# Rounding of the weights with two VectorE operations, loads spread over the first units, two buffers of scores

## The chip, the cores and the metric

The kernel runs on one core of a Trainium2 chip. The metric is the device time of one execution in microseconds (us), as the median of several runs. Engines are named as in the profile: PE (TensorE, matmuls; PEld is its weight load), DVE (VectorE), ACT (ScalarE), POOL (GpSimd), SP (SyncE, which issues all DMAs here).

## The reference

Attention in which each query keeps its 32 largest scores, then a feed-forward block with a gated activation. The weights come in 64-bit floats, everything else in 32-bit.

```python
B, H, S, D = 8, 8, 576, 64
scores = q @ k.T / sqrt(D)
kth = 32nd largest score of each row
attn = softmax(where(scores >= kth, scores, -1e9))
x = (attn @ v)                      # to (B*S, H*D) = (4608, 512)
g = x @ w_gate                      # (512, 1536)
val = x @ w_val                     # (512, 1536)
out = (g * sigmoid(g) * val) @ w_out   # (1536, 512)
```

## The kernel before, in words

**Units.** The attention is cut into 160 units (`units`): for each of 8 batches, five query tiles (four of 128 rows, the last of 64), each for four pairs of heads. A unit of the first four tiles holds two heads side by side (128 x 1152 scores; "full unit"); one of the last tile holds both heads on the two halves of the partitions (128 x 576; "one-head unit").

**Stages of a unit.** `scores` multiplies on PE into four PSUM tiles and ACT copies them to `sc` (L261, or L247 for one-head units). `select` finds the 32nd largest on DVE in four rounds of eight: MAX8 (L277), then MATCH_REPLACE8 (L281) that blanks the found eight in `rest`; a compare (L287) writes the penalty `e`. `penalize` adds `sc` to `e` on POOL (L299). `weigh` takes exp on ACT with the row sum `tot` (L308); `normalize` adds a small constant and inverts `tot` on DVE (L318, L320) and scales `e` on ACT (L323). `turn` transposes `e` on PE (L335, nine 128 x 128 transposes, in groups of 5 and 4 with a piece of other work between them) and ACT copies the result to `et` (L336). `values` multiplies with V on PE (L355, L364) and ACT copies to `xT` (L379).

**The loop.** One iteration of the last loop treats four units at once: top-k of unit n, scores of unit n+1, penalty and exp of unit n-1, transposes of unit n-2, product with V of unit n-3. The Q/K slabs of a pair are prepared (`fetch`, `prep`) two units ahead. Instructions run on each of PE, DVE, ACT and POOL in exactly the order in which the loop writes them: the end of the kernel ties each to the one before it on its engine. SP has its own queue of DMAs, in program order too.

**The feed-forward block** runs over 18 blocks of 256 rows (`feed`). It is cut into pieces (`piece`): four matmuls with w_gate or w_val (L418), or two with w_out (L452). `credit` lets 4.6 pieces into a full unit and 2.3 into a one-head unit, as far as rows are ready. What follows a product on ACT (`gate`: tanh, a halved copy, plus one, L436 to L438, called the tanh trio in the text; `value`: a copy, L443) and on POOL (L439, L444) waits in the lists `on_act` and `on_pool` and is written out at `flush`.

**Rounding of the weights.** PE multiplies weights that are rounded from 64-bit floats by integer operations on the two 32-bit words of each (`rounded`). There are 72 pieces of 128 x 256. `weights` runs them as a pipeline of steps; in each step one piece has its DMA issued (L96), another, three steps behind, passes POOL's clamp (L102) and ACT's scaling and Abs (L107, L109), another, four behind, two DVE operations (L114, L117) and POOL's add (L121), and one five behind the last DVE operation (L124). `rounding(k)` runs k steps; `need` runs as many as a product asks for. The loop calls it with 5 steps in units 0 to 9 and 4 after that.

**Buffers.** `sc` has three buffers (L229), `e` three, `rest` one, the DMA tiles `w` four, `m` three. Scores, transposes, slabs and products with V share a pool of five PSUM tiles (`ps_t`), in rotation.

**Start.** Before the loop come K and Q of pair 0, three rounding steps, K and Q of pair 1, then for all four pairs K, Q (where not loaded) and V.

Of the kernel before, what the change touches and what calls it, by code (L numbers as in the profile page):

```python
# [15 lines left out]
P = 128  # L16
# [4 lines left out]
BLK = 256  # L21
WP = 256
HUGE = 122880.0
LEAST = 3.4332275390625e-05


@with_exitstack
def kernel(
# [63 lines left out]
    def rounded(src, dst):  # L92

        n = dst.shape[1]
        w = ffn.tile([P, n, 2], I32, tag="w", name="w", bufs=4)
        nc.sync.dma_start(w[:], src.bitcast(I32).rearrange("p (f t) -> p f t", t=2))  # L96
        yield
        low, high = w[:, :, 0], w[:, :, 1]


        hi = conv.tile([P, n], FP32, tag="hi", name="hi")
        nc.gpsimd.tensor_scalar(  # L102
            hi[:], high.bitcast(FP32), HUGE, -HUGE, ALU.min, ALU.max
        )

        ulps = conv.tile([P, n], I32, tag="ulps", name="ulps")
        nc.scalar.mul(ulps[:], low.bitcast(U32), 2.0**-29)  # L107
        size = conv.tile([P, n], FP32, tag="size", name="size")
        nc.scalar.activation(size[:], hi[:], AF.Abs)  # L109
        yield  # L110

        hi = hi[:].bitcast(I32)
        bits = conv.tile([P, n], I32, tag="bits", name="bits")
        nc.vector.tensor_scalar(  # L114
            bits[:], hi, 3, 0x3FFFFFFF, ALU.logical_shift_left, ALU.bitwise_and
        )
        nc.vector.scalar_tensor_tensor(  # L117
            out=bits[:], in0=hi, scalar=-0x40000000, in1=bits[:],
            op0=ALU.bitwise_and, op1=ALU.bitwise_or,
        )  # L120
        nc.gpsimd.tensor_tensor(bits[:], bits[:], ulps[:], ALU.add)  # L121
        yield

        nc.vector.scalar_tensor_tensor(  # L124
            out=dst, in0=size[:], scalar=LEAST, in1=bits[:].bitcast(FP32),
            op0=ALU.is_ge, op1=ALU.mult,
        )

    def weights():

        pieces = []
        for f in range(0, DFF, WP):
            for src, dst in ((w_gate, wg), (w_val, wv)):
                for c in range(KC):
                    pieces.append((src[c * P : (c + 1) * P, f : f + WP], dst[:, c, f : f + WP]))
        for c in range(MC):
            for f in range(0, DM, WP):
                pieces.append((w_out[c * P : (c + 1) * P, f : f + WP], wo[:, c, f : f + WP]))
        pieces = [rounded(*p) for p in pieces]
        for n in range(len(pieces) + 5):  # L140
            for lag in (5, 4, 3, 0):
                if 0 <= n - lag < len(pieces):
                    next(pieces[n - lag], None)
            ready[0] = max(n - 4, 0)
            yield

    ready = [0]
# [2 lines left out]
    def rounding(n):  # L150
        for _ in range(n):
            next(weight, None)

    def need(n):

        while ready[0] < n:
            next(weight)
# [68 lines left out]
    def scores(n):  # L226
        b, qt, hp = units[n]
        slab = preps[b * NHP + hp]
        sc = work.tile([P, 2 * S], FP32, tag="sc", name="sc", bufs=3)  # L229
        halves = [slice(0, D), slice(D, P)]  # L230
        half = S // 2

        def bank():
            return ps_t.tile([P, 512], FP32, tag="t", name="s")


        if qt == J:
            banks = [bank() for _ in range(2)]
            for i, ps in enumerate(banks):
                for d in halves:  # L240
                    k0 = R + i * half
                    nc.tensor.matmul(  # L242
                        ps[d, 0:half], slab[d, S + R : S + 2 * R], slab[d, k0 : k0 + half]
                    )
            yield
            for i, ps in enumerate(banks):
                nc.scalar.copy(sc[:, i * half : (i + 1) * half], ps[:, 0:half])  # L247
        else:
            q0 = S + 2 * R + qt * P
            banks = []  # L250
            for i in range(2):
                for hh, d in enumerate(halves):
                    ps = bank()
                    banks.append((i + 2 * hh, ps))
                    k0 = (1 - hh) * R + i * half
                    nc.tensor.matmul(  # L256
                        ps[:, 0:half], slab[d, q0 : q0 + P], slab[d, k0 : k0 + half]
                    )
            yield
            for i, ps in banks:  # L260
                nc.scalar.copy(sc[:, i * half : (i + 1) * half], ps[:, 0:half])  # L261
        state[n] = dict(sc=sc)

    def select(n):

        nh = n_heads(units[n][1])
        sc = state[n]["sc"]
        m = small.tile([P, 2, TOP_K], FP32, tag="m", name="m")
        heads = [slice(t * S, (t + 1) * S) for t in range(nh)]
        rest = work.tile([P, 2 * S], FP32, tag="rest", name="rest", bufs=1)  # L270
        e = work.tile([P, 2 * S], FP32, tag="e", name="e", bufs=3)
        state[n] |= dict(m=m, e=e, heads=heads)
        cur = sc
        rounds = TOP_K // 8
        for r in range(rounds):
            for t, hs in enumerate(heads):
                nc.vector.max(m[:, t, 8 * r : 8 * r + 8], cur[:, hs])  # L277
            yield
            if r < rounds - 1:
                for t, hs in enumerate(heads):  # L280
                    nc.vector.match_replace(  # L281
                        rest[:, hs], m[:, t, 8 * r : 8 * r + 8], cur[:, hs], LOWEST
                    )
                cur = rest
                yield
        for t, hs in enumerate(heads):
            nc.vector.tensor_scalar(  # L287
                e[:, hs], sc[:, hs], m[:, t, TOP_K - 1 : TOP_K], FAR, ALU.is_lt, ALU.mult
            )
# [114 lines left out]
    def feed(kb):  # L404
# [7 lines left out]
        def product(w, s, then):  # L412
            ps = ps_f.tile([P, 2, BLK], FP32, tag="f", name="f")
            need(8 * s + (4 if w is wg else 8))
            for i in range(2):
                m = 2 * s + i
                for c in range(KC):
                    nc.tensor.matmul(  # L418
                        ps[:, i, :],
                        w[:, c, m * P : (m + 1) * P],  # L420
                        x[:, c, :],
                        start=(c == 0),
                        stop=(c == KC - 1),
                    )
                if i == 1:
                    on_act.append(lambda: then(ps))
                yield
# [20 lines left out]
        for t in range(BLK // P):  # L448
            ps = ps_f.tile([P, DM], FP32, tag="f", name="o_ps")
            for m in range(MC):  # L450
                need(8 * MS + 2 * m + 2)
                nc.tensor.matmul(  # L452
                    ps[:],
                    hs[m // 2][:, m % 2, t * P : (t + 1) * P],
# [51 lines left out]
    def run(steps):  # L506
        for _ in steps:
            pass

    load(0)  # L510
    rounding(3)
    load(1)
    for i in range(NHP):
        if i > 1:
            load(i)
        load_v(i)
    run(fetch(0))
    run(scores(0))
    run(fetch(1))
    credit = [0.0]  # L520
    no = iter(())
    over = {}
    for n in range(NU + 3):
        topk = select(n) if n < NU else no
        over[n - 1] = normalize(n - 1) if 0 <= n - 1 < NU else no
        nxt = scores(n + 1) if n + 1 < NU else no
        turned = turn(n - 2) if 0 <= n - 2 < NU else no
        ahead = fetch(n + 2) if n + 2 < NU else no
        if n < NU:
            credit[0] = min(credit[0] + (2.3 if units[n][1] == J else 4.6), 8.0)  # L530
        flush(on_act)
        if 0 <= n - 1 < NU:
            penalize(n - 1)
        run(over.pop(n - 2, no))
        flush(on_pool)
        if n >= 3:
            values(n - 3)
            b, qt, hp = units[n - 3]
            if qt == J and b + 1 < B:
                load_v((b + 1) * NHP + hp)  # L540
        next(nxt, None)
        next(topk, None)
        next(topk, None)
        rounding(1 + (n < 2 * NHP + 2))
        pieces(1)
        next(nxt, None)
        next(turned, None)
        flush(on_act)
        pieces(1)
        next(turned, None)  # L550
        flush(on_act)
        if 0 <= n - 1 < NU:
            weigh(n - 1)
        flush(on_pool)
        next(topk, None)
        next(topk, None)
        rounding(1)
        next(ahead, None)
        pieces(1)
        next(ahead, None)  # L560
        next(topk, None)
        rounding(1)
        next(over[n - 1], None)
        pieces(1)
        next(topk, None)
        rounding(1)
        next(over[n - 1], None)
        next(topk, None)
        next(topk, None)
        pieces(6)  # L570
    while piece():
        pass
# [48 lines left out]
```

## Time and profile before

| | |
|---|---|
| median of 3 runs | 1973.31 us (1972.61 to 1979.06) |
| the profiled execution | 1975.04 us |
| its span in the profile | 1973.2 us |
| busy PE | 1779.5 us (90%) |
| busy DVE | 1640.1 us (83%) |
| busy ACT | 1156.0 us (59%) |
| busy POOL | 773.0 us (39%) |
| mean granted PE clock | 0.942 |

The page cuts the span into 40 equal slices and gives the busy share of each engine in tenths, and the PE clock granted by the throttle in tenths of full speed. A row of the timeline gives start, length, engine, line, operation, output and inputs, the number of instructions merged into it, and in brackets the idle time before it and what ended that. A row of the waits gives who waited for whom: total us, times, longest.

### The profile page before, as it was taken

What the parts mean: (1) busy time and instruction counts of PE and PEld (TensorE: products, weight loads), DVE (VectorE), ACT (ScalarE), POOL (GpSimd) and SP (SyncE); (2) the same over time, 40 slices, a digit from 0 to 9 for tenths busy, and PEclk for the clock granted to TensorE, in tenths of its full rate; (3) what the DMA queues carried; (4) which work ended last, traced back from release to release, by engine and by line L of the source; (5) the groups of instructions that cost most, each with busy time, mean ns of one, the idle gap of its engine ahead of it and who ended that gap; (6) DMA issues with size and microseconds to landing.
All of it is one profiled execution on the core that took longest, in us unless ns stands there. A gap on an engine that the chain in (4) does not pass through costs nothing.

```text
span 1973.2 us, 29487 instructions
## 1 busy us (share of the span) xinstructions
PE 1779.5 (90%) x10144; PEld 1297.7 (66%) x10144; DVE 1640.1 (83%) x3708; ACT 1156.0 (59%) x2821; POOL 773.0 (39%) x686
## 2 busy tenths in 40 slices
PE   3444779989999999999999999989999999899899
PEld 1223655847686867686768686858686867586666
DVE  5999687998889998989799898998898988889700
ACT  3555455656575656666667566656675656565512
POOL 2555453424334434343434352434343434243412
PEclk6566789999999999999999999999999999999999
DMA  5222111100030002100030002000120002000000
GB/s 153 84 80 75 43 50 43 44 12 1 9 79 11 1 12 57 30 1 11 4 78 7 12 2 68 18 11 1 33 54 11 1 14 50 11 1 11 1 11 11
DMA packets 111253, 59.58 MB, mean 30 GB/s; under 512 B 89088, under 2 KB 97280, under 8 KB 111104
## 3 DMA queue, kind: packets, MB, share of 16 engines
q1 hardware_dynamic: 111104, 57.70, 11.1%
q8 instruction: 80, 1.31, 0.3%
q14 instruction: 69, 0.57, 0.1%
HBM read 48.23 MB, written 9.44 MB: 29 GB/s over the span
## 4 chain that ended last, share of the span: by engine, by line
PE 78%; DVE 13%; issue 3%; ACT 3%; POOL 2%; SPq 1%; DMA 1%; POOLq 0%; ACTq 0%; DVEq 0%
PE f L418 37%; PE o_ps L452 18%; PE av L364 7%; PE etps L335 6%; PE s L256 6%; DVE m L277 5%; DVE rest L281 4%; PE s L242 2%; PE av L355 1%; PE kqps L211 1%; DVE bits L117 1%; DVE e L287 1%; DVE bits L114 1%; ACT e L308 1%; POOL bits L121 1%
## 5 line engine op out<-in xcount | busy, mean ns | idle before, releaser
L299 POOL TENSOR_TENSOR e<-e,sc 128x1152 f32<-128x1152 f32 (+1 forms) x160 | 383.0, 2394 | 731.3 <-DVE e L287 487.1
L277 DVE MAX8 m<-rest 128x8 f32<-128x576 f32 x864 | 613.7, 747 | 2.2
L418 PE MATMUL f<-xT,wg 128*128 128x256 f32 x1728 | 423.1, 391 | 16.7 <-ACT xT L379 16.7
L281 DVE MATCH_REPLACE8 rest<-m,rest 128x576 f32<-128x576 f32 x576 | 423.9, 743 | 0.0
L418 PE MATMUL f<-xT,wv 128*128 128x256 f32 x1728 | 409.3, 384 | 0.0
L452 PE MATMUL o_ps<-wo,h 128*128 128x512 f32 x864 | 400.1, 599 | 4.4 <-DVE wo L124 4.4
L418 PEld LDWEIGHTS f<-xT,wg 128*128 128x128 f32 x1728 | 323.4, 194 | 89.7 <-issue 27.8
L336 ACT COPY et<-etps 128x512 f32<-128x512 f32 (+1 forms) x448 | 195.1, 477 | 305.8 <-PE etps L335 305.2
L418 PEld LDWEIGHTS f<-xT,wv 128*128 128x128 f32 x1728 | 321.0, 193 | 48.3 <-issue 9.9
L335 PE MATMUL etps<-ident,e 128*128 128x128 f32 (+1 forms) x1312 | 207.4, 289 | 122.2 <-ACT sc L261 70.5
L335 PEld LDWEIGHTS etps<-ident,e 128*128 128x128 f32 (+1 forms) x1312 | 168.0, 148 | 202.8 <-issue 99.1
L323 ACT ACTIVATE e<-e,tot 128x576 f32<-128x576 f32 x288 | 209.5, 770 | 133.7 <-DVE tot L320 133.7
L452 PEld LDWEIGHTS o_ps<-wo,h 128*128 128x128 f32 x864 | 153.6, 190 | 163.6 <-issue 156.0
L439 POOL TENSOR_TENSOR h<-h,half_g 128x512 f32<-128x512 f32 x108 | 137.9, 1277 | 265.3 <-ACT h L438 258.8
L308 ACT ACTIVATE e<-e,bias 128x576 f32<-128x576 f32 x288 | 221.6, 776 | 4.1 <-POOL e L299 4.1
L277 DVE MAX8 m<-sc 128x8 f32<-128x576 f32 x288 | 205.1, 749 | 10.1 <-ACT sc L261 10.1
L281 DVE MATCH_REPLACE8 rest<-m,sc 128x576 f32<-128x576 f32 x288 | 212.0, 743 | 0.0
L256 PE MATMUL s<-kqT 64*128 64x288 f32 x1024 | 172.7, 459 | 11.4 <-ACT kqT L216 11.3
L364 PE MATMUL av<-et,v 128*64 128x128 f32 (+1 forms) x2560 | 178.5, 281 | 2.1 <-ACT et L336 1.0
L261 ACT COPY sc<-s 128x288 f32<-128x288 f32 x512 | 167.2, 416 | 12.8 <-PE s L256 12.3
L318 DVE TENSOR_SCALAR tot<-tot 128x2 f32<-128x2 f32 (+1 forms) x160 | 25.4, 159 | 168.0 <-ACT e L308 168.0
L444 POOL TENSOR_TENSOR h<-h,val 128x512 f32<-128x512 f32 x108 | 139.1, 1288 | 60.7 <-ACT val L443 60.3
(45 smaller groups left out, 1459.8 us busy)
## 6 DMA issues: line engine op xcount, KB each, us to landing
kq_in<-in_k_dram SPq DMA_DIRECT2D x64, 128.0 KB, 2.8
kq_in<-in_q_dram SPq DMA_DIRECT2D x64, 128.0 KB, 3.0
v<-in_v_dram SPq DMA_DIRECT2D x32, 256.0 KB, 3.0
w<-in_moe_w_gate_dram SPq DMA_DIRECT2D x24, 256.0 KB, 2.7
w<-in_moe_w_val_dram SPq DMA_DIRECT2D x24, 256.0 KB, 2.7
w<-in_moe_w_out_dram SPq DMA_DIRECT2D x24, 256.0 KB, 2.5
out_dram<-o SPq DMA_DIRECT2D x40, 128.0 KB, 2.4
out_dram<-o SPq DMA_DIRECT2D x16, 256.0 KB, 2.4
```

The lines of the kernel that those rows point to most:

```text
L256: nc.tensor.matmul(ps[:, 0:half], slab[d, q0 : q0 + P], slab[d, k0 : k0 + half])
L261: nc.scalar.copy(sc[:, i * half : (i + 1) * half], ps[:, 0:half])
L277: nc.vector.max(m[:, t, 8 * r : 8 * r + 8], cur[:, hs])
L281: nc.vector.match_replace(rest[:, hs], m[:, t, 8 * r : 8 * r + 8], cur[:, hs], LOWEST)
L299: nc.gpsimd.tensor_tensor(e[:, every], e[:, every], sc[:, every], ALU.add)
L308: nc.scalar.activation(e[:, hs], e[:, hs], AF.Exp, bias=bias[:, t : t + 1], scale=scale, accum_out=tot[:, t : t + 1],)
L323: nc.scalar.mul(e[:, hs], e[:, hs], tot[:, t : t + 1])
L335: nc.tensor.transpose(ps[0:kl, c * P : (c + 1) * P], e[:, k0 : k0 + kl], ident[:])
L336: nc.scalar.copy(et[0:kl, c0 : c0 + cn, :], ps[0:kl, 0 : cn * P].rearrange("p (c j) -> p c j", c=cn),)
L364: nc.tensor.matmul(av[hh * R : (hh + 1) * R, 0:ql], v_last[:, hh, :] if c == J else vt[:, hh, c, :], moving, start=last and c == 0, stop=c ...
L418: nc.tensor.matmul(ps[:, i, :], w[:, c, m * P : (m + 1) * P], x[:, c, :], start=(c == 0), stop=(c == KC - 1),)
L452: nc.tensor.matmul(ps[:], hs[m // 2][:, m % 2, t * P : (t + 1) * P], wo[:, m, :], start=(m == 0), stop=(m == MC - 1),)
```

## The change

1. `rounded` uses two DVE operations instead of three. Abs on ACT comes first, on the DMA's tile; POOL clamps the absolute value from both sides (the lower bound, now 2^-15, replaces the last compare); DVE shifts and masks; POOL adds; the last DVE operation takes sign and top bit from the DMA's tile and joins them. It comes six steps behind the DMA (before: five). `w` has seven buffers instead of four, `bits` three instead of two.
2. A rounding step follows every third top-k operation of one head (`dve`), where before steps stood at fixed places; top-k operations are now written out head by head. Four steps instead of three come before the loop.
3. K and Q of pairs 2 and 3 and the V tiles are loaded in the first units instead of ahead of the loop.
4. `sc` has two buffers instead of three, and `m` two instead of three.
5. A flush of both lists stands before the seventh step (m == 6) of the product with w_out.

```diff
-LEAST = 3.4332275390625e-05
+LEAST = 3.0517578125e-05
...
     def rounded(src, dst):
         n = dst.shape[1]
-        w = ffn.tile([P, n, 2], I32, tag="w", name="w", bufs=4)
+        w = ffn.tile([P, n, 2], I32, tag="w", name="w", bufs=7)
         nc.sync.dma_start(w[:], src.bitcast(I32).rearrange("p (f t) -> p f t", t=2))
         yield
         low, high = w[:, :, 0], w[:, :, 1]
-        hi = conv.tile([P, n], FP32, tag="hi", name="hi")
-        nc.gpsimd.tensor_scalar(
-            hi[:], high.bitcast(FP32), HUGE, -HUGE, ALU.min, ALU.max
-        )
+        size = conv.tile([P, n], FP32, tag="size", name="size")
+        nc.scalar.activation(size[:], high.bitcast(FP32), AF.Abs)
+        nc.gpsimd.tensor_scalar(size[:], size[:], HUGE, LEAST, ALU.min, ALU.max)
         ulps = conv.tile([P, n], I32, tag="ulps", name="ulps")
         nc.scalar.mul(ulps[:], low.bitcast(U32), 2.0**-29)
-        size = conv.tile([P, n], FP32, tag="size", name="size")
-        nc.scalar.activation(size[:], hi[:], AF.Abs)
         yield
-        hi = hi[:].bitcast(I32)
-        bits = conv.tile([P, n], I32, tag="bits", name="bits")
+        bits = conv.tile([P, n], I32, tag="bits", name="bits", bufs=3)
         nc.vector.tensor_scalar(
-            bits[:], hi, 3, 0x3FFFFFFF, ALU.logical_shift_left, ALU.bitwise_and
-        )
-        nc.vector.scalar_tensor_tensor(
-            out=bits[:], in0=hi, scalar=-0x40000000, in1=bits[:],
-            op0=ALU.bitwise_and, op1=ALU.bitwise_or,
+            bits[:], size[:].bitcast(I32), 3, 0x3FFFFFFF,
+            ALU.logical_shift_left, ALU.bitwise_and,
         )
         nc.gpsimd.tensor_tensor(bits[:], bits[:], ulps[:], ALU.add)
         yield
         nc.vector.scalar_tensor_tensor(
-            out=dst, in0=size[:], scalar=LEAST, in1=bits[:].bitcast(FP32),
-            op0=ALU.is_ge, op1=ALU.mult,
+            out=dst.bitcast(I32), in0=high, scalar=-0x40000000, in1=bits[:],
+            op0=ALU.bitwise_and, op1=ALU.bitwise_or,
         )
...
-            for lag in (5, 4, 3, 0):
+            for lag in (6, 4, 3, 0):
...
-        sc = work.tile([P, 2 * S], FP32, tag="sc", name="sc", bufs=3)
+        sc = work.tile([P, 2 * S], FP32, tag="sc", name="sc", bufs=2)
...
-        m = small.tile([P, 2, TOP_K], FP32, tag="m", name="m")
+        m = small.tile([P, 2, TOP_K], FP32, tag="m", name="m", bufs=2)
...
             for t, hs in enumerate(heads):
                 nc.vector.max(m[:, t, 8 * r : 8 * r + 8], cur[:, hs])
-            yield
+                yield
             if r < rounds - 1:
                 for t, hs in enumerate(heads):
                     nc.vector.match_replace(
                         rest[:, hs], m[:, t, 8 * r : 8 * r + 8], cur[:, hs], LOWEST
                     )
+                    yield
                 cur = rest
-                yield
...
                 need(8 * MS + 2 * m + 2)
+                if m == 6:
+                    flush(on_act)
+                    flush(on_pool)
...
     load(0)
-    rounding(3)
+    rounding(4)
     load(1)
-    for i in range(NHP):
-        if i > 1:
-            load(i)
-        load_v(i)
...
+        def dve(k):
+            for _ in range(k * nh):
+                next(topk, None)
+                due[0] += 1 / 3
+                if due[0] >= 1:
+                    due[0] -= 1
+                    rounding(1)
...
         next(nxt, None)
-        next(topk, None)
-        next(topk, None)
-        rounding(1 + (n < 2 * NHP + 2))
+        dve(1)
+        if 2 <= n + 2 < NHP:
+            load(n + 2)
+        if n < NHP:
+            load_v(n)
+        dve(1)
         pieces(1)
         next(nxt, None)
         next(turned, None)
...
-        next(topk, None)
-        next(topk, None)
-        rounding(1)
+        dve(2)
         next(ahead, None)
         pieces(1)
         next(ahead, None)
-        next(topk, None)
-        rounding(1)
+        dve(1)
         next(over[n - 1], None)
         pieces(1)
-        next(topk, None)
-        rounding(1)
+        dve(1)
         next(over[n - 1], None)
-        next(topk, None)
-        next(topk, None)
+        dve(1)
+        run(topk)
         pieces(6)
```

## The prediction

> **What bounds the kernel now.** I read the page's slices first, then the waits of the first 320 us, then the timeline of a few units in the middle, and last the per-stretch windows around the places where the PE clock falls.
>
> ```profile
> PE   3444779989999999999999999989999999899899
> ...
> DVE  5999687998889998989799898998898988889700
> ...
> PEclk6566789999999999999999999999999999999999
> ```
>
> One slice is 49.3 us. In slices 2 to 4 DVE is full and PE is 40% busy at half clock: top-k and weight rounding on DVE set the pace. From about 330 us on PE is full, with DVE at 90% beside it.
>
> ```profile
> ACT size L109 <- POOL hi L102: 120.1, 59, 5.5
> PEld etps L335 <- ACT sc L261: 75.1, 13, 7.3
> ```
>
> These are waits of the first 320 us (total, times, longest). ACT stands for POOL's clamp of the rounding, and its copies of the next scores stand behind that; PE's transposes of e wait for these copies, because the fifth transpose writes a PSUM bank that the scores filled (5 banks in rotation, 8 used per unit).
>
> The middle of the kernel, in order of time, for one full unit (two heads):
>
> ```profile
> 611.52 0.17 DVE L318 TENSOR_SCALAR tot<-tot 128x2 f32<-128x2 f32 x1 [1.86 <-ACT e L308]
> 614.44 0.94 DVE L287 TENSOR_SCALAR e<-sc,m 128x576 f32<-128x576 f32 x2
> 615.52 2.63 POOL L299 TENSOR_TENSOR e<-e,sc 128x1152 f32<-128x1152 f32 x1 [3.96 <-DVE e L287]
> 615.97 1.31 ACT L261 COPY sc<-s 128x288 f32<-128x288 f32 x4 [0.40 <-PE s L256]
> 618.17 0.71 PE L335 MATMUL etps<-ident,e 128*128 128x128 f32 x5
> ...
> 621.56 0.78 ACT L308 ACTIVATE e<-e,bias 128x576 f32<-128x576 f32 x1
> 623.22 0.17 DVE L318 TENSOR_SCALAR tot<-tot 128x2 f32<-128x2 f32 x1 [0.97 <-ACT e L308]
> ```
>
> I call the end of DVE's e (615.38) the unit's start T. ACT copies new scores at 615.97, while POOL still adds the old scores into e until 618.15. Three score buffers allow that.
>
> **The change, part by part.** The sum is made on the profiled execution, 1975.0 us (span 1973.2 and 1.8 around it); the median of the three runs, 1973.3, is 1.7 below it.
>
> *Rounding, start-up.* A step is three DVE operations now:
>
> ```profile
> 140.45 0.41 DVE L124 SCALAR_TENSOR_TENSOR wg<-size,bits 128x256 f32<-128x256 f32 x1
> 140.78 0.28 DVE L114 TENSOR_SCALAR bits<-hi 128x256 int32<-128x256 int32 x1
> 141.10 0.42 DVE L117 SCALAR_TENSOR_TENSOR bits<-hi,bits 128x256 int32<-128x256 int32 x1
> ```
>
> By their starts 0.33 each, 1.0 a step; the new step is 0.66. A full unit without rounding is 10.63 (e ends at 1056.24, 1066.88 and 1077.51 below). Units 1 to 9 take 17.03 now with five steps. With 14/3 = 4.67 steps they take 10.63 + 4.67 x 0.66 = 13.7, plus what POOL blocks: steps now fall after the first, second or third operation of a unit, into POOL's e (T+0.15 to T+2.78). The nearest row is this one, issued while POOL's e ran:
>
> ```profile
> 213.15 2.72 DVE L117 SCALAR_TENSOR_TENSOR bits<-hi,bits 128x256 int32<-128x256 int32 x1
> ```
>
> It took 2.72 instead of 0.42. A step at T+0.7, T+1.35 or T+2.05 would so lose 2.1, 1.4 or 0.7, mean 1.4: 15.1 a unit. Gain (17.03 - 15.1) x 9 = 17; bounds 30 (nothing blocked) and 0.
>
> *Loads unit by unit.* Unit 0 lasts from 11.50 to 35.51 now, with 9.8 us in which DVE waits for weights whose DMAs stand on SP's queue behind three pairs' K, Q and all V (issued at 28.72). In the new order the queue holds K, Q of pair 0, four weight pieces, pairs 1 and 2, V of pair 0, then weights again at about 17. Against it, the fourth rounding step puts an Abs and a scaling ahead of ACT's first slab copy, waiting for the first weight piece (POOL started on it at 8.21; the copy now starts at 5.59): first top-k 1.8 later, at 13.3. Then 10.2 of top-k, six rounding operations at 0.33 and 1 us of small waits: ends at 26.5. Gain 9; bounds 5 and 11. K, Q of pair 3 and the later V are issued 5 to 15 us before use: nothing.
>
> *Units 10 to 15.* They take 120.0 us (188.8 to 308.8). ACT waits there 4 us a unit for POOL's clamp and copies scores at T+5.5 to T+6.9. ACT's Abs now comes first and waits for a DMA alone, so in two units of three the copies can start when POOL's e ends, T+2.8; in the third a scaling waits for a POOL add of the step before, as late as now. The rest of the loop (product, tanh, POOL's h, POOL's bits, DVE) stays. Gain 2 x 6 = 12; bounds 0 and 20. Final operations come at distance 6 instead of 5: no cost, only buffers. Rounding left over in units 16 to 19 is 3 steps, in one-head units with DVE slack: 0 to 2.
>
> Start-up in sum: 17 + 9 + 12 = 38 saved, bounds 5 and 60.
>
> *Two score buffers, the whole rest.* Scores of unit n+2 now go where unit n's lie, and POOL's e of unit n must have read them. So ACT's copy waits until T + 0.15 + 2.63 = T+2.78; a copy takes 0.42; PE's fifth transpose can start at T+3.25, not earlier. Behind the waiting copy stand ACT's et copies, the tanh trio or val, and exp; PE waits for the copy, and DVE's tot for exp. From that transpose (618.17 + 4 x 0.11 = 618.61) to DVE's tot (623.22) are 4.61, from tot to the next T 3.86 (611.52 to 615.38). That is a loop: 3.25 + 8.47 = 11.7 a unit. It is closed anew only through this wait; today the same fifth transpose often runs at T+0.5 to T+2. Whether 11.7 costs depends on PE's own load from transposes to transposes:
>
> ```profile
> 1056.36 0.71 PE L335 MATMUL etps<-ident,e 128*128 128x128 f32 x5
> 1068.59 0.71 PE L335 MATMUL etps<-ident,e 128*128 128x128 f32 x5
> 1079.10 0.71 PE L335 MATMUL etps<-ident,e 128*128 128x128 f32 x5
> ...
> 1065.95 0.93 DVE L287 TENSOR_SCALAR e<-sc,m 128x576 f32<-128x576 f32 x2
> 1076.58 0.93 DVE L287 TENSOR_SCALAR e<-sc,m 128x576 f32<-128x576 f32 x2
> ```
>
> 12.23 with five FFN pieces, 10.51 with four. What ACT does between the copies lengthens the loop: val between transposes and exp 0.5 (12.2), the tanh trio there 1.5 (13.2), the trio ahead of the third et copy, pushed late by the later score copies, 0.8 (12.5, my estimate from copy 1.3, et 0.75, trio 1.6). I sorted the 112 full units from 341 to 1858 us in the timeline by load and loop:
> - load 10.5: 17 with 11.7, 14 with 12.2 to 12.5, 10 with 13.2: 20 + 26.5 + 27 = 73
> - load 12.2: 8 with 13.2, 26 with 12.2 to 12.5: 8 + 3 = 11; the other loads of 12.2 and the long ones (17 us): 0
> - 11 units where PE idles today: 17; the one-head units, with POOL's e of 1.4: 6
>
> Sum 107. Bounds: 60 (half of the estimates, nothing where PE idles) and 107. Nothing can win it back: the order of PE's work is written out and is the same in both kernels.
>
> *The clock after the new stalls.* 31 of these stalls of PE are over 1.9 us.
>
> ```profile
> 832.00:835.10 3.10, 1.21 (x9) 0.95 (x9) 3.10 (x6) 3.10 (x10) 1.05 (x1) 1.00 0.02 6
> 835.10:841.90 6.80, 6.53 (x30) 4.67 (x31) 6.80 (x18) 2.33 (x7) 1.77 (x2) 0.50 0.00 0
> 449.40:456.20 6.80, 4.38 (x25) 3.26 (x22) 6.80 (x16) 3.52 (x10) 1.65 (x1) 1.00 0.00 0
> ```
>
> (Stretch, length, busy PE, PEld, DVE, ACT, POOL, granted clock.) 1.9 us idle within 3.1 were followed by 6.8 us at half clock, worth 3.4 us of PE; 2.4 us idle, spread wider, by nothing. Bounds 0 and 31 x 3.4 = 105; nearest to the second row, three drops, 10. The Trainium skill (TensorE: Matmul & The Clock Gate, Part 1: The HAM clock gate) says that the clock falls after at least one idle window of about 3.4 us; by that no stall here would drop it, the term would be 0 and the time 10 us lower. The row at 835 disagrees with it.
>
> *The rest.* The flush at m == 6 leaves the order of POOL and PE as it is; two buffers of m make the first max wait for POOL's bias of two units earlier, done 10 us before: 0. The stores and PE's tail after 1872 are untouched: 0.
>
> Sum: 1975.0 - 38 + 107 + 10 = 2054; 1.7 less for the median: 2052.
>
> **Rivals.** (A) Faster: the wait for POOL's e is hidden, since PE reaches its fifth transpose after T+3.25 anyway. Then only start-up counts: 1975 - 38 - 2 = 1935. For it: in 51 of the 112 full units PE is that late today. Against: in 43 of the others it comes by T+2.05, and between ACT's exp and DVE's tot the chain in the middle has no slack. It decides where the loop of 11.7 stays below PE's load, which 12.2 does and 10.5 doesn't. (B) The clock: PE's stalls drop it in most cases; 20 of 31 at 3.4 us: 2054 + 58 = 2110. For it the row at 835. (C) The rounding does not shorten start-up, since every second operation it keeps meets POOL's e or h: gain 10 instead of 38: 2080. (D) Loop and start-up cancel: gain 55, loop 60: 1980.
>
> **How the numbers follow.** Forecast 0.55 (2052), B 0.12, C 0.12, D 0.08, A 0.13. Low end: beside D's 1980, some 15 for a loop shorter still, 1965, leaves A out. High end: 2115 takes in B. Less than 0.3% (6 us) from no change is about what a measurement of this kernel cannot tell. Of D half falls within or below it: faster 0.15, same 0.04, slower 0.81.
>
> **What would show it.** Right: ACT's sc copies waiting for POOL's e in some hundred units; e ends of full units 11.7 or more apart, hardly any at 10.63 after 350 us; PE etps waiting for ACT sc for some 90 us in all after 330 us; unit 10 starting near 163, PE full from near 295 on. Wrong: etps without such waits and units still at 10.63 (A); PEclk at 6 to 8 in the middle slices (B); unit 10 starting after 180 (C).

## The result and the profile after

The changed kernel takes 2033.88 us (median of 4, 2032.71 to 2034.60) against 1974.11 us before: 59.8 us slower, a ratio of 1.0298 with an interval of 1.0279 to 1.0317. Forecast were 2052 us, range 1965 to 2115. Line numbers in this part are those of the kernel that each view belongs to; in the changed kernel the copy of scores is L255 (before L261), POOL's e L293 (L299), the transposes L329 (L335).

The page's slices of the changed kernel; one is 50.8 us:

```profile
PE   4447889889999999898999999989999999898999
...
DVE  7998988978888878787888888887888878878700
...
PEclk7668889899999999999999999989999999999989
```

DVE is full in slices 2 and 3 where it was in 2 to 4, so the start is over sooner. From slice 8 on, however, PE is at 8 in seven slices (before in four), and DVE nearly always at 8 or 7. Neither is full throughout, which fits a loop through several engines. The chain of waits says the same: PE has 58% of it where it had 78%, and POOL, before at 2%, has 8%.

```profile
PE 58%; DVE 20%; ACT 10%; POOL 8%; issue 3%; SPq 0%; DMA 0%; POOLq 0%; DVEq 0%; ACTq 0%
```

The waits between 300 and 1930 us of the changed kernel (who waited for whom, total us, times, longest):

```profile
ACT sc L255 <- POOL e L293: 260.9, 108, 3.6
DVE tot L312 <- ACT e L302: 253.0, 128, 7.1
...
PE etps L329 <- ACT sc L255: 87.5, 54, 3.0
```

The first and third of these waits are new: from 300 us to the last unit of before, no score copy waits for POOL's e, and the transposes wait for score copies 1.5 us in all. One unit shows them in order of time (timeline of the changed kernel):

```profile
1148.29 0.93 DVE L281 TENSOR_SCALAR e<-sc,m 128x576 f32<-128x576 f32 x2
...
1149.33 0.60 PE L329 MATMUL etps<-ident,e 128*128 128x128 f32 x4
1149.40 2.62 POOL L293 TENSOR_TENSOR e<-e,sc 128x1152 f32<-128x1152 f32 x1 [4.03 <-DVE e L281]
...
1152.06 1.31 ACT L255 COPY sc<-s 128x288 f32<-128x288 f32 x4 [3.31 <-POOL e L293]
...
1152.51 0.47 PE L329 MATMUL etps<-ident,e 128*128 128x128 f32 x1 [2.58 <-ACT sc L255]
...
1160.19 0.17 DVE L312 TENSOR_SCALAR tot<-tot 128x2 f32<-128x2 f32 x1 [4.09 <-ACT e L302]
```

T (end of DVE's e) is 1149.22. POOL adds until 1152.02, only then ACT copies scores (T+2.84), and PE's fifth transpose, which ran on the heels of the fourth in the kernel before, starts at T+3.29. Between the fourth transpose and the fifth PE does nothing for 2.58 us.

The trace gives this account of the two kernels (T1, T10 and so on: the start T of that unit, which is the end of DVE's e of the unit before it, us):

| | T1 | T10 | T16 | T20 | T159 | T20 to T159 |
|---|---|---|---|---|---|---|
| before | 35.59 | 188.83 | 308.82 | 341.93 | 1865.41 | 1523.5 |
| after | 25.04 | 159.22 | 266.85 | 300.71 | 1925.18 | 1624.5 |

By unit 20 the changed kernel is 41.2 us ahead; from there to the start of the last unit, T159, it loses 101.0.

### The profile page after: what moved, and what is told of

The parts are those of the page before. It is cut to its first block, busy times and chain, and to the rows that moved or that the text cites. A ratio compares the mean times of both kernels' runs of the same rounds, so it can differ in the third digit from the quotient of the medians.

```text
span 2031.9 us, 29366 instructions
## 1 busy us (share of the span) xinstructions
PE 1798.8 (89%) x10144; PEld 1302.0 (64%) x10144; DVE 1636.4 (81%) x3636; ACT 1153.2 (57%) x2821; POOL 770.2 (38%) x686
## 4 chain that ended last, share of the span: by engine, by line
PE 58%; DVE 20%; ACT 10%; POOL 8%; issue 3%; SPq 0%; DMA 0%; POOLq 0%; DVEq 0%; ACTq 0%
PE f L412 27%; PE o_ps L449 14%; POOL e L293 8%; DVE rest L275 7%; DVE m L271 6%; PE etps L329 6%; PE av L358 4%; PE s L250 4%; ACT e L302 4%; DVE e L281 4%; ACT et L330 2%; ACT sc L255 1%; PE s L236 1%; DVE bits L110 1%; PE kqps L205 1%
## 5 line engine op out<-in xcount | busy, mean ns | idle before, releaser
L293 POOL TENSOR_TENSOR e<-e,sc 128x1152 f32<-128x1152 f32 (+1 forms) x160 | 381.9, 2387 | 735.0 <-DVE e L281 624.8
L329 PE MATMUL etps<-ident,e 128*128 128x128 f32 (+1 forms) x1312 | 223.0, 294 | 183.7 <-ACT sc L255 133.2
L412 PEld LDWEIGHTS f<-xT,wv 128*128 128x128 f32 x1728 | 322.4, 194 | 49.0 <-issue 10.7
L329 PEld LDWEIGHTS etps<-ident,e 128*128 128x128 f32 (+1 forms) x1312 | 170.8, 148 | 277.1 <-ACT sc L255 151.6
L255 ACT COPY sc<-s 128x288 f32<-128x288 f32 x512 | 167.4, 412 | 292.7 <-POOL e L293 289.1
L330 ACT COPY et<-etps 128x512 f32<-128x512 f32 (+1 forms) x448 | 200.2, 500 | 127.7 <-PE etps L329 127.6
L250 PE MATMUL s<-kqT 64*128 64x288 f32 x1024 | 171.4, 456 | 14.7 <-ACT kqT L210 14.7
```

What stands on the lines that cost most here:

```text
L250: nc.tensor.matmul(ps[:, 0:half], slab[d, q0 : q0 + P], slab[d, k0 : k0 + half])
L293: nc.gpsimd.tensor_tensor(e[:, every], e[:, every], sc[:, every], ALU.add)
L329: nc.tensor.transpose(ps[0:kl, c * P : (c + 1) * P], e[:, k0 : k0 + kl], ident[:])
L330: nc.scalar.copy(et[0:kl, c0 : c0 + cn, :], ps[0:kl, 0 : cn * P].rearrange("p (c j) -> p c j", c=cn),)
L412: nc.tensor.matmul(ps[:, i, :], w[:, kc, m * P : (m + 1) * P], x[:, kc, :], start=(kc == 0), stop=(kc == KC - 1),)
```

## The experiments

The theory: the two score buffers close a loop over DVE, POOL, ACT and PE, and cost what is lost after unit 20; the rounding and the loads give the gain at the start. The rivals: the loss comes from another part (top-k head by head, two buffers of m, the flush), or the clock makes most of it; and the gain of the start could be another's too.

**1. Three score buffers in the changed kernel.** `w` and `bits` have fewer buffers, to make room for it, and the DMA of a piece is issued one step later, its last rounding operation one step earlier (`lags`). The control has these changes alone.

```diff
-        w = ffn.tile(..., bufs=7)
+        w = ffn.tile(..., bufs=5)
-        bits = conv.tile(..., bufs=3)
+        bits = conv.tile(...)
-        lags = (6, 4, 3, 0)
+        lags = (5, 4, 3, 1)
-        sc = work.tile(..., bufs=2)       # not in the control
+        sc = work.tile(..., bufs=3)       # not in the control
```

> The changed kernel with three buffers of scores again. To make room, the DMA tiles are five instead of seven: the weight's DMA is issued one step later and the last rounding operation comes five steps behind the start instead of six. Main theory (the loop through POOL's e): ACT's score copies no longer wait, e ends of full units are 10.63 apart again where DVE leads, the 101 us lost between units 20 and 159 come back, the start keeps most of its 42 us: 1930 to 1945. Rival (the loss comes from two buffers of m, the top-k written head by head, or the flush): stays above 2020. Second rival (the clock does it): in between, with the same number of half-clock stretches.

> Control for the run before: only the shorter DMA and rounding distances (five DMA tiles), two buffers of scores as in the changed kernel. All theories: the rounding ends with unit 16, so nothing changes after that; the start loses 0 to 10 us where a last rounding operation now waits for a POOL add of the step before: 2034 to 2044.

With three buffers 1929.70 us, 0.9777 of before (0.9762 to 0.9792); the control 2030.23, 1.0284 (1.0269 to 1.0300). The third buffer alone is worth 100.5 us. The smaller buffers and the shorter lag cost nothing by themselves: the control is 3.7 us (0.2%) below the change, where no gain was expected. The rivals "head by head", "two buffers of m" and "flush" fall: all three are still in the three-buffer kernel, which is 43.7 us faster than before and takes 1525.2 us from T20 to T159, where the kernel before takes 1523.5. So does the clock as a cause of its own: with the third buffer there are 6 stretches at half clock between T20 and T159, with two (the control) 14. The score copies in the page of the three-buffer kernel, and of the changed kernel (busy, mean ns of one, idle just before them, what ended most of it):

```profile
L255 ACT COPY sc<-s 128x288 f32<-128x288 f32 x512 | 167.2, 417 | 13.0 <-PE s L250 12.5
```

```profile
L255 ACT COPY sc<-s 128x288 f32<-128x288 f32 x512 | 167.4, 412 | 292.7 <-POOL e L293 289.1
```

The copies take as long, but the 289 us of waiting for POOL are gone. And the timeline of the three-buffer kernel has them beside POOL's e again, with the transposes ahead of POOL's end (1070.58 against 1069.16 + 2.63 = 1071.79):

```profile
1068.08 0.93 DVE L281 TENSOR_SCALAR e<-sc,m 128x576 f32<-128x576 f32 x2
1068.43 1.30 ACT L255 COPY sc<-s 128x288 f32<-128x288 f32 x4
1069.16 2.63 POOL L293 TENSOR_TENSOR e<-e,sc 128x1152 f32<-128x1152 f32 x1 [8.88 <-DVE e L281]
1070.58 0.71 PE L329 MATMUL etps<-ident,e 128*128 128x128 f32 x5
```

**2. Two score buffers in the kernel before**, nothing else.

```diff
-        sc = work.tile([P, 2 * S], FP32, tag="sc", name="sc", bufs=3)
+        sc = work.tile([P, 2 * S], FP32, tag="sc", name="sc", bufs=2)
```

> The kernel before with two buffers of scores and nothing else. Main theory: the whole loop cost between units 20 and 159, about 100 us, and nothing in units 1 to 14, where the copies come 3 to 5 us after POOL's e anyway: 2065 to 2080, the slowest of all. Rival (two buffers of scores are harmless): 1974.

2073.95 us, 1.0506 (1.0488 to 1.0523): 100.5 us more than before, the same as in the first pair. From T20 to T159 it takes 1624.5 us, to the tenth what the changed kernel takes. Its waits from 340 us on hold the new wait with almost the same total:

```profile
ACT sc L261 <- POOL e L299: 260.4, 107, 3.3
```

So going from three buffers to two costs the same with and without the rest of the change.

**3. The loads alone; the rounding alone; both with three buffers.** The first is the kernel before with K and Q of pairs 2 and 3 and V loaded in the first units. The second is the kernel before with the new `rounded` of the diff (and `w`, `bits`, lags as in the control), its steps called where they were before. The third is the two together: rounding and loads of the change, without its head-by-head order, its steps after every third top-k operation, the two buffers of `sc` and `m`, and the flush.

```diff
     load(1)
-    for i in range(NHP):
-        if i > 1:
-            load(i)
-        load_v(i)
...
         next(topk, None)
+        if 2 <= n + 2 < NHP:
+            load(n + 2)
+        if n < NHP:
+            load_v(n)
         next(topk, None)
         rounding(1 + (n < 2 * NHP + 2))
```

> The kernel before with the loads alone moved: K and Q of pairs 2 and 3 and all V tiles in the first units, everything else as it was (three operations a rounding step, three score buffers). Theory: DVE no longer waits 9.8 us in unit 0 for the weights' DMAs, unit 1 starts near 26 instead of 35.5, and as DVE then runs at its old pace the gain is carried to the end: 9 to 11 us saved, 1963. Rival (the wait only moves to a later DMA or transpose): within 3 us of 1973.

> The kernel before with the new two-operation rounding alone (DMA issued one step in, last operation five steps behind, five DMA tiles); places of the steps, loads and three score buffers as before. By the prediction's prices: units 1 to 9 take 10.63 + 5 x 0.66 = 13.9, some 14.3 with small waits, 25 us saved; units 10 to 15 save 12; unit 0 still waits for the weights' DMAs: 1974 - 37 = 1937. Rival (what POOL and ACT do per step bounds the start, not DVE): 15 us saved or less, 1959 or more.

> The two-operation rounding at the old fixed places, the loads unit by unit, three buffers of scores: the parts of the change that should gain, without the new places of the steps and without the shared score buffers. If the parts add up: 1920.7 less 9 to 11 = 1911. Beside the run with three buffers and all else changed (1929.7), the difference is then the price of a step after every third top-k operation: about 19 us, most of it in units 10 to 15. Rival (places don't matter, the earlier start did): 1925 or more.

The medians of before in these comparisons, 1973.4 us, are of its own runs beside each of them.

| | median | ratio to before | T1 | units 1 to 9, each | units 10 to 15, each |
|---|---|---|---|---|---|
| before | 1973.4 | | 35.59 | 17.03 | 20.00 |
| loads alone | 1964.88 | 0.9953 (0.9938 to 0.9968) | 25.89 | 17.02 | 19.66 |
| rounding alone | 1920.69 | 0.9731 (0.9717 to 0.9746) | 36.76 | 14.69 | 14.27 |
| both, three buffers | 1909.34 | 0.9676 (0.9661 to 0.9690) | 25.02 | 14.69 | 14.14 |
| the change | 2033.88 | 1.0298 (1.0279 to 1.0317) | 25.04 | 14.91 | 17.94 |

The loads shorten unit 0 and little else, the rounding the units 1 to 15 and not unit 0; their gains add (8.5 + 52.7 = 61.2 against 64.0 measured). Both together is the fastest kernel of this study, 64 us below before and 124.5 below the change. In its slices (47.7 us each) PE is first full in slice 6, and stays so from slice 9 on but for single 8s:

```profile
PE   4448899799999999899999999989999999999899
```

The loads came near what was expected, and the two together within 2 us of it. The rounding alone did not: 1937 was expected. Units 1 to 9 gave 21 us instead of 25, so the surprise is in units 10 to 15: at the old fixed places the new rounding saves (20.00 - 14.27) x 6 = 34 us there, in the change 12.

**4. No rounding step early in a unit.** The three-buffer kernel of experiment 1, but no step before the fourth top-k operation, so that hardly one meets POOL at work on e.

```diff
+        ops = [0]
...
             for _ in range(k * nh):
                 next(topk, None)
+                ops[0] += 1
                 due[0] += 1 / 3
-                if due[0] >= 1:
+                if due[0] >= 1 and ops[0] >= 4:
```

> The run with three score buffers and all else changed, but no rounding step before the fourth top-k operation of a unit, so that none meets POOL's e (the steps due earlier come at the fourth). Theory (a DVE rounding operation that meets a POOL add stands until it ends): units 1 to 9 fall from 15.0 on average to 13.9, 10 us saved, some more in units 10 to 15: 1912 to 1922. Rival (it is the number of steps that counts, or waits for POOL's results): 1930 as with three buffers.

1915.65 us, 0.9706 (0.9690 to 0.9722), 14.0 less than with the steps after every third operation. Units 1 to 9 take 14.02 each instead of 14.92, units 10 to 15 15.99 instead of 17.18. Most of the reason is in two groups, the first of the changed kernel, the second of this one (DVE's last rounding operation during units 1 to 9; ns min/median/max):

```profile
L117 DVE SCALAR_TENSOR_TENSOR wg<-w,bits x22: 397/408/2446, 25.6 to 156.4; 128x256 int32<-128x256 int32 x22
```

```profile
L117 DVE SCALAR_TENSOR_TENSOR wg<-w,bits x21: 399/409/746, 27.9 to 146.2; 128x256 int32<-128x256 int32 x21
```

The same operation with the same median takes up to 2.45 us in the change and 0.75 here. Summed over units 1 to 9, nine rounding operations lost 13.2 us in the change (13.3 in experiment 1), three lost 1.0 here; of these 12.3 us the units got only 8.1 shorter. In units 10 to 15 the blocked operations lost 14.7 us in experiment 1 and 6.1 here, 8.6 less, which covers the 7.1 saved there. What still separates 15.99 from the 14.14 of the fixed places was not tried: the places of the steps still differ, and the order head by head, two buffers of `m`, four steps ahead of the loop and the flush lie between the two.

**5. Two buffers, given back by halves.** The changed kernel with a score tile for each head and POOL's add in two halves, so that the first half of a buffer is free when POOL is done with the first head.

```diff
-        sc = work.tile([P, 2 * S], FP32, tag="sc", name="sc", bufs=2)
+        sc = [
+            work.tile([P, S], FP32, tag=f"sc{t}", name=f"sc{t}", bufs=2)
+            for t in range(n_heads(qt))
+        ]
...
-        every = slice(0, nh * S)
-        nc.gpsimd.tensor_tensor(e[:, every], e[:, every], sc[:, every], ALU.add)
+        for t, hs in enumerate(heads):
+            nc.gpsimd.tensor_tensor(e[:, hs], e[:, hs], sc[t][:], ALU.add)
```

> The changed kernel with two buffers of scores, but a tile of its own for each head, and POOL's add in two halves of 576: ACT's first copy then waits only for the first half, T + 0.15 + 1.4, and PE's fifth transpose can start at T+2.0 instead of T+3.25. Theory of the loop: it shrinks by 0.9 to 1.2 us a unit (ACT's other copies, which wait for the second half, become late next), of the 101 us some 45 to 60 come back: 1975 to 1990. Rival (two buffers cost in another way than by the end of POOL's e): 2030 and more, as POOL has one instruction more a unit.

1951.22 us, 0.9885 (0.9870 to 0.9899): faster than before, and below the range expected. T20 to T159 takes 1545.9, so 79 of the 101 us came back. The wait is still there, and more often; from 295 us on:

```profile
ACT sc L259 <- POOL e L297: 217.3, 183, 1.9
```

Its total is 83% of that in the change, and yet most of the loss is gone. What PE feels of it has shrunk more: its transposes wait 28.6 us for score copies there, in the change 87.5. The timeline shows how:

```profile
1124.62 0.93 DVE L285 TENSOR_SCALAR e<-sc,m 128x576 f32<-128x576 f32 x2
1125.21 2.98 POOL L297 TENSOR_TENSOR e<-e,sc 128x576 f32<-128x576 f32 x2 [4.00 <-DVE e L285]
1126.85 0.40 ACT L259 COPY sc<-s 128x288 f32<-128x288 f32 x1
1127.91 0.71 PE L333 MATMUL etps<-ident,e 128*128 128x128 f32 x5
1128.22 1.00 ACT L259 COPY sc<-s 128x288 f32<-128x288 f32 x3 [0.97 <-POOL e L297]
```

The one copy that the fifth transpose needs goes at T+1.30 (T is 1125.55); the other three wait for POOL's second half until T+2.67. PE turns all five from 1127.91 on without a wait. This fits a loop that is made of the first copy's wait, while less hangs on the other three, which the expectation had priced in the loop as well; no run takes the two waits apart.

## Why the prediction was right

**The start: forecast 38 saved, measured 42.0 by unit 16** (41.2 by unit 20). Unit 0: 10.55 earlier at T1 (forecast 9; the first max begins at 12.97, forecast 13.3). Units 1 to 9: (17.03 - 14.91) x 9 = 19.1 (forecast 17, from 15.1 a unit). The share of it that was a guess, 1.4 us for each blocked step, came as 13.2 us for nine operations, 1.5 each. A step that meets POOL's e, in the changed kernel's timeline; POOL adds from 69.83 to 72.44:

```profile
69.61 0.75 DVE L271 MAX8 m<-sc 128x8 f32<-128x576 f32 x1
70.28 2.45 DVE L117 SCALAR_TENSOR_TENSOR wg<-w,bits 128x256 int32<-128x256 int32 x1
72.65 0.28 DVE L110 TENSOR_SCALAR bits<-size 128x256 int32<-128x256 int32 x1
```

Units 10 to 15: 12.4 (forecast 12). This agreement is worth less than it looks. Experiment 3 shows 34 for the same rounding at fixed places, above the forecast's bound of 20. So the term was right by luck, by two errors that cancel: the rounding is worth more there than was thought, and the rest of the change gave 22 back. Of these, 9 are the blocked operations (14.2 us in the change, 4.8 in the kernel with both parts at the old places); the forecast counted them for units 1 to 9 and left them out of units 10 to 15. Some 4 more are the two score buffers (17.78 a unit in the control, 17.18 with three buffers). The other 9 were not taken apart.

**The loop: forecast 107, and 10 for the clock; measured 101.0 together.** The mechanism was right. Its steps are seen one by one: the copies at T+2.8 in 90 of 111 units, the fifth transpose at T+3.2 to T+3.4 in 81 of 112 and earlier in two, 108 waits of the copies ("some hundred"), 87.5 us of PE ("some 90"), and of the 108 full units from 24 to 155 only 3 follow the one before by less than 10.7 us, where 49 did. By the forecast's own classes, measured from fifth transpose to fifth transpose, with the clock's drops in it:

| PE's load / loop forecast | units | forecast | measured |
|---|---|---|---|
| 10.5 / 11.7 | 17 | 20 | 18.1 |
| 10.5 / 12.2 to 12.5 | 14 | 26.5 | 18.0 |
| 10.5 / 13.2 | 10 | 27 | 21.8 |
| 12.2 / all | 46 | 11 | 15.3 |
| long loads (17 us) | 6 | 0 | 5.1 |
| units where PE idled | 11 | 17 | 15.3 |
| one-head units | 27 | 6 | 7.3 |

(Eight full units whose load fits no row are left out; the rows add up to 100.9.)

The first three rows, 57.9 us against the forecast's 73.5, are where the loop was mis-sized, and their means hide why. In 34 of these 41 units the loop came close to the forecast: 11.5 to 11.8 us in 15 units (forecast 11.7), 12.2 in the three with val between transposes and exp (12.2), 12.0 to 12.2 in the eight with the trio ahead of the third et copy (12.5), 13.2 in eight (13.2). The other seven came 10.41 or 10.45 us apart, exactly as in the kernel before. All seven end in an iteration in which ACT copies the scores of a one-head unit, and there PE does not wait (the changed kernel, unit 36):

```profile
497.15 2.64 POOL L293 TENSOR_TENSOR e<-e,sc 128x1152 f32<-128x1152 f32 x1 [7.73 <-DVE e L281]
498.52 0.71 PE L329 MATMUL etps<-ident,e 128*128 128x128 f32 x5
499.82 0.70 ACT L241 COPY sc<-s 128x288 f32<-128x288 f32 x2 [3.23 <-POOL e L293]
```

The copies (L241) wait for POOL's e here too, but PE has turned all five before; from 300 us on the transposes wait 0.7 us in all for L241 (their weight loads, three times), and 87.5 for L255. So the mis-sized term is the number of units that the loop binds: the forecast gave these seven the full loop, some 13 us. The trio ahead of the third et copy, an estimate, was 0.4 too long in eight units, 3 us more.

**The clock: forecast three more drops, measured eight.** Between T20 and T159 there are 13 stretches at half clock (71.7 us in all), before 5 (27.3 us). The stall of 1149 shown above is one, and a unit with the same work and no drop stands beside it (windows of the changed kernel: length, busy PE, PEld, DVE, ACT, POOL, granted clock):

```profile
1149.00:1152.20 3.20, 0.93 (x7) 0.60 (x5) 3.20 (x8) 0.14 (x1) 2.80 (x2) 1.00 0.00 0
1152.20:1155.60 3.40, 3.09 (x8) 2.55 (x9) 3.40 (x8) 1.82 (x6) 1.05 (x1) 0.50 0.00 0
1149.20:1164.00 14.80, 12.22 (x69) 9.93 (x67) 10.71 (x26) 7.63 (x18) 5.30 (x4) 0.88 0.00 0
1560.30:1573.60 13.30, 10.73 (x70) 8.77 (x68) 10.73 (x25) 7.63 (x18) 5.31 (x4) 1.00 0.00 0
```

14.80 us against 13.30: 1.5 for the drop; other such pairs differ by up to 2.5. Eight more drops are then, as an estimate, 12 to 20 of the 101.0 us, and the loop itself 81 to 89. That the term came within twice its size is luck again. The forecast had 31 stalls of over 1.9 us and let three of them drop the clock, at 3.4 us each. There are 17 such waits of the transposes between T20 and T159; with ten of them, a stretch at half clock begins during the wait or at most 1.1 us after it, one more lies within such a stretch already, and six dropped nothing. That share is nearer to rival B's (20 of 31) than to the forecast's; the term stayed small because long waits were fewer and each drop cost 1.5 to 2.5. The half clock of the second row follows 2.27 us without work within 3.2, so the row speaks once more against the rule of the Trainium skill (TensorE: Matmul & The Clock Gate, Part 1: The HAM clock gate), by which it takes an idle window of about 3.4 us. Why ten of these waits drop the clock and six do not, among them one of 2.57 us in the unit at 1560, stays open.

**The sum.** 1975.0 - 41.2 + 101.0 - 1.7 = 2033.1, against 2033.9 measured. The forecast was 18 us high: 3 of the start and 16 of the loop with its clock, less 1 by which this sum falls short.

**The rivals.** A (wait hidden) fell: PE waits. It would have been right about the start, as 1929.70 in experiment 1 shows against its 1935. B fell by its time, 2110 us; from slice 8 on PEclk is at 8 in three slices and at 9 in the others. C fell: unit 10 starts at 159.2, not after 180. D was wrong in the loop, 101 and not 60.

## What to carry to other kernels

Count the buffers of a tile along the whole way of its last reader, not of the engine that reads it first: here the last reader was an add on POOL, an engine with 2% of the chain of waits in the kernel before, and one buffer less turned it into a loop of four engines that cost 100 us in 1500. A change of several parts is best read by its parts: 42 us of gain at the start were outweighed by one number (`bufs=2`), and undoing it gave the better kernel. The total of a wait is not its price; halving the piece that is given back left 83% of the waiting and took away 78% of the loss.

## What was not expected of the hardware

Not that a rounding operation of DVE stands still while POOL adds (the row at 70.28; the forecast had one such row), but that the top-k operations in the same place do not. In the unit at 1149 of the changed kernel, MATCH_REPLACE8 takes its 0.74 us within POOL's 2.62. Over the whole trace of that kernel, none of 370 MAX8 that began during a TENSOR_TENSOR of POOL took more than 0.77 us.

```profile
1149.14 1.41 DVE L271 MAX8 m<-sc 128x8 f32<-128x576 f32 x2
...
1150.53 0.74 DVE L275 MATCH_REPLACE8 rest<-m,sc 128x576 f32<-128x576 f32 x1
```

So where on DVE a step is put can cost more than what it does: 14 us between experiments 1 and 4 from places alone, with the same instructions.
